# One change in six parts to an attention and mixer kernel: per-pair mixer, FFN halves queued apart, program order for two batches, mask by matmul, loads by need

## The chip, the core and the metric

The kernel runs on one core of a Trainium2 chip. The metric is the device time of one execution in microseconds (us). Every timed run carries a state, fast or slow (slow: over 1.5% above the fastest of its kernel), and only fast runs are compared. "Before" and "after" are the kernels without and with the change; e1 to e18 are experiments.

## The reference, cut to what matters

Eight batches, eight heads, 576 positions, head size 64. Attention with a causal mask and a bias from a running sum comes first. Its output is laid out as `x` (576 x 512 for each batch). A low-rank mixer along the sequence and a two-layer FFN follow.

```python
scores = q @ k.T * scale + min(bias, 0)        # causal: -1e9 above the diagonal
attn   = softmax(scores)
x      = (attn @ v).transpose(0, 2, 1, 3).reshape(B, S, H * D)
u      = x + ((x.T @ U) @ V).T                  # U: 576 x 32, V: 32 x 576
out    = u + relu(u @ w_ch1) @ w_ch2            # 512 -> 2048 -> 512
```

## The kernel before

Work is cut into 32 head pairs, four to a batch, and nine FFN blocks of 512 tokens. For each pair `scores(n)` makes the exponentials and `values(n)` the attended values in `x_sb`. Once per batch `seqmix(b)` turns `x_sb` into `u`, held transposed as `uT`. `chanmix(g)` is one FFN block: a wide half (`relu(u @ w_ch1)`) and a narrow half. The FFN is the filler. It waits in a queue, and one of its steps is put after each step of attention, so that TensorE (PE) has something to do while the others work on the softmax.

Queries and keys of pairs 4 and up come in groups of two pairs. A group is loaded by GpSimd's queue into `qk_sd`, then `place(g)` turns it: four stream transposes on VectorE (DVE) into `turned`, then eight copies by DMA into a slot. This is called "the turn". Group g serves pairs 2g and 2g+1.

```python
def place(g):                                   # "the turn" of group g
    slot = slots[g % NSLOT]
    nc.sync.dma_start(out=slot[D:KA, ...], in_=rows_hbm[...])
    src = qk_t.pop(g)
    turned = work.tile([128, 2, 2, S], BF16, tag="turned", name="turned")
    for e in range(2):
        for c in range(2):
            nc.vector.transpose(turned[:, e, c]..., src[:, c]...)          # L172, 4 in all
        for a in range(4):
            nc.sync.dma_start(out=slot[ds(32 * e, 32), a, 0 : 2 * S], ...)  # L177, 8 in all

def seqmix(b):                                  # once per batch
    x_sb = x_of.pop(b)
    up = pwork()
    for t in range(5):
        nc.tensor.matmul(up, lhsT=U_sb[:, t, :], rhs=x_sb[:, t, :], ...)   # L266, 512 columns
    ux = work.tile([128, DM], BF16, tag="ux", name="ux")
    nc.vector.tensor_copy(ux, up)
    yield
    for dt in range(4):
        ...                                     # x_sb transposed + V.T @ ux, then copied to uT
        yield
    ...

    # the end of the program: the opening is in program order, the rest is not
    with tc.manual_schedule():
        ...                                     # loads, set-up, batch 0, spin matmuls (48)
        warmly(seqmix(0))
    place(2)
    fill.append(chanmix(0))
    fill_with(8)
    for n in range(PB, NP + 1):                 # PB = 4 pairs in a batch, NP = 32
        b, hp = divmod(n, PB)
        if hp == 0 and b + 1 < B:
            load_qk(b + 1)
            load_v(b + 1)
        if hp % 2 == 0 and n + 2 < NP:
            place(n // 2 + 1)                   # two pairs ahead
        if n < NP:
            run(scores(n))                      # one filler step after each step
        if n > PB:
            run(values(n - 1))
            if hp == 0:
                run(seqmix(b - 1))
                fill.append(chanmix(b - 1))
    ...
```

Inside `tc.manual_schedule()` every engine gets its instructions in the order of the program. Outside, a scheduler chooses the order on each engine when the kernel is built. "Program order" means the former, "the scheduler" the latter. The spin matmuls are useless ones that keep PE busy in the opening.

The softmax here doesn't subtract the row's maximum and nothing guards it: scores larger than these inputs give would overflow.

Of the kernel before, what the change touches and what calls it, by code (L numbers as in the profile page):

```python
# [20 lines left out]
def kernel(  # L21
# [52 lines left out]
    identity = consts.tile([128, 128], BF16)  # L74
    PW = 1664
# [26 lines left out]
    def load_qk(b):  # L102
        for g in range(2 * b, 2 * b + 2):
            qk_t[g] = loads.tile([128, 2, ST * D], BF16, tag="qk_sd", name="qk_sd", bufs=3)
            for c, src in enumerate((q, k)):
                for a in range(4):
                    nc.gpsimd.dma_start(  # L107
                        out=qk_t[g][ds(32 * a, 32), c, :].rearrange("p (n f) -> p n f", n=6),
                        in_=src[b, 4 * (g % 2) + a].rearrange("(n p t) d -> p n (t d)", p=32, t=3),
                    )  # L110
# [71 lines left out]
    def scores(n):  # L182
        pT = pTs[n % 2]
        tail = pscore()
        for hh in range(2):
            qT = head_of(n, hh)[0:KA, 0:S]
            kT = head_of(n, hh)[0:KA, S:]

            def mm(dst, j, lo, hi):
                nc.tensor.matmul(  # L190
                    dst,
                    lhsT=kT[:, ds(j * 128, 128)],
                    rhs=qT[:, lo:hi],
                    start=True,
                    stop=True,
                )

            diag = pscore()
            for j in range(4):
                mm(diag[:, ds(j * 128, 128)], j, j * 128, j * 128 + 128)  # L200
            nc.scalar.activation(pT[:, hh, 0:512], diag, EXP, scale=scale)  # L201
            nc.vector.tensor_tensor(  # L202
                pT[:, hh, 0:512], pT[:, hh, 0:512], keep.rearrange("p a b -> p (a b)"), op=ALU.min
            )
            mm(tail[:, ds(hh * 64, 64)], 4, 512, S)
            yield
            far = pscore()
            mm(far[:, 0:448], 0, 128, S)
            mm(far[:, 448:512], 3, 512, S)
            nc.scalar.activation(pT[:, hh, 512:1024], far, EXP, scale=scale)  # L210
            mid = pscore()
            mm(mid[:, 0:320], 1, 256, S)
            mm(mid[:, 320:512], 2, 384, S)
            nc.scalar.activation(pT[:, hh, 1024:1536], mid, EXP, scale=scale)  # L214
            if hh == 1:
                nc.scalar.activation(
                    pT[:, :, 1536:1600],
                    tail[:, 0:128].rearrange("p (a b) -> p a b", a=2),
                    EXP,
                    scale=scale,  # L220
                )
                nc.vector.tensor_tensor(  # L222
                    pT[:, :, 1536:1600], pT[:, :, 1536:1600], keep[:, 0:2, 0:64], op=ALU.min
                )
            yield
# [36 lines left out]
    def seqmix(b):  # L262
        x_sb = x_of.pop(b)
        up = pwork()
        for t in range(5):
            nc.tensor.matmul(  # L266
                up,
                lhsT=U_sb[:, t, :],
                rhs=x_sb[:, t, :],
                start=(t == 0),  # L270
                stop=(t == 4),
            )
        ux = work.tile([128, DM], BF16, tag="ux", name="ux")
        nc.vector.tensor_copy(ux, up)
        yield
        for dt in range(4):
            ut = pwork()
            for t in range(4):
                nc.tensor.matmul(  # L279
                    ut[:, ds(t * 128, 128)],  # L280
                    lhsT=x_sb[:, t, ds(dt * 128, 128)],
                    rhs=identity,
                    start=(t == 0),
                    stop=False,
                    skip_group_check=True,
                )
            nc.tensor.matmul(  # L287
                ut,
                lhsT=ux[:, ds(dt * 128, 128)],
                rhs=V_sb[:, 0:512],  # L290
                start=False,
                stop=True,
                skip_group_check=True,
            )
            nc.vector.tensor_copy(uT[:, dt, ds(b * S, 512)], ut)  # L295
            yield
        ut = pwork()
        for dt in range(4):
            nc.tensor.matmul(
                ut[:, ds(dt * 64, 64)],  # L300
                lhsT=x_sb[:, 4, ds(dt * 128, 128)],
                rhs=identity[:, :64],
                start=True,
# [3 lines left out]
            nc.tensor.matmul(  # L307
                ut[:, ds(dt * 64, 64)],
                lhsT=ux[:, ds(dt * 128, 128)],
                rhs=V_sb[:, 512:S],  # L310
                start=False,
                stop=True,
                skip_group_check=True,
            )
        nc.vector.tensor_copy(
            uT[:, :, ds(b * S + 512, 64)], ut[:, 0:256].rearrange("p (a b) -> p a b", a=4)
        )
        yield

# [3 lines left out]
    def chanmix(g):  # L323
        hT = work.tile([128, NF, 512], BF16, tag="hT", name="hT")
        for nf in range(NF):
# [10 lines left out]
            yield  # L336
        for i in range(4):
# [36 lines left out]
    def run(gen):  # L374
        for _ in gen:
            step_fill()
# [8 lines left out]


    copy_a, copy_v = nc.scalar.copy, nc.vector.tensor_copy
    with tc.manual_schedule():
# [4 lines left out]
        load_first(4, 4)  # L393
        nc.gpsimd.memset(keep, 3.0e38)
# [9 lines left out]
        ones(warm)  # L404
        ones(rows[:, 0:3, 0, :])
        ones(rows[:, 3, 1, :])
        for slot in slots:
            nc.vector.memset(slot[:KA, :, 2 * S :], 0.0)
        idle = pwork()

        def spin(n):
            for _ in range(n):
                nc.tensor.matmul(idle, lhsT=warm[:, 0:128], rhs=warm, start=True, stop=True)  # L413

        spin(10)
        chain = first_transposes(0, (copy_a, copy_a))
        nc.vector.tensor_scalar(s_sb, s_sb, 0.0, 1.0 / scale, op0=ALU.max, op1=ALU.mult)
        nc.vector.tensor_tensor_scan(cum, s_sb, s_sb, 0.0, op0=ALU.add, op1=ALU.max)
        next(chain)
        spin(2)  # L420
        nc.scalar.mul(rows[:, 3, 0, :], cum, -1.0)
        drain(chain)
        spin(2)
        rest = s_sb
        nc.vector.tensor_copy(rows[:, 0, 1, :], cum)
        nc.vector.tensor_sub(rest, cum, rows[:, 0, 1, :])
        nc.vector.tensor_copy(rows[:, 1, 1, :], rest)
        nc.vector.tensor_sub(rows[:, 2, 1, :], rest, rows[:, 1, 1, :])
        for h in range(H):
            nc.sync.dma_start(  # L430
                out=slots[h // 4][D:KA, h % 4, 0 : 2 * S],
                in_=rows[h : h + 1].rearrange("n r c s -> n r (c s)"),
            )
        nc.sync.dma_start(
            out=rows_hbm[:, ds(2 * PB, BH - 2 * PB)].rearrange("r n c s -> n r c s"),
            in_=rows[2 * PB :],
        )
        for i, vt in enumerate(v_slots):
            nc.vector.memset(vt[:, :, :, D : D + 1], 1.0)
            nc.vector.memset(vt[64:, 4, :, :], 0.0)  # L440
            if i == 0:
                drain(first_transposes(1, (copy_a, copy_v)))
                spin(8)
        nc.vector.memset(U_sb, 0.0)
        nc.vector.memset(V_sb, 0.0)
        for pT in pTs:
            nc.vector.memset(pT[:, :, 1600:], 1.0)
        load_v(0)
        nc.gpsimd.dma_start(
            out=U_sb[:, :4, :R], in_=moe_U[:512].rearrange("(kt kp) r -> kp kt r", kp=128)  # L450
        )
        nc.gpsimd.dma_start(out=U_sb[:64, 4, :R], in_=moe_U[512:576])
        nc.gpsimd.dma_start(out=V_sb[:R], in_=moe_V)
        load_w1(0)
        load_w1(1)
        load_qk(1)
        load_w1(2)
        load_w1(3)
        load_v(1)
        for i in range(4):  # L460
            load_w2(i)
# [4 lines left out]

        drain(scores(0))
        warmly(first_transposes(2, (copy_v, copy_v)))
        drain(scores(1))
        warmly(first_transposes(3, (copy_v, copy_v)))  # L470
        warmly(values(0))
        warmly(scores(2))
        warmly(values(1))
        warmly(scores(3))
        warmly(values(2))
        warmly(values(3))
        warmly(seqmix(0))
    place(2)
    fill.append(chanmix(0))
    fill_with(8)  # L480
    for n in range(PB, NP + 1):
        b, hp = divmod(n, PB)
        if hp == 0 and b + 1 < B:
            load_qk(b + 1)
            load_v(b + 1)
        if hp % 2 == 0 and n + 2 < NP:
            place(n // 2 + 1)
        if n < NP:
            run(scores(n))
        if n > PB:  # L490
            run(values(n - 1))
            if hp == 0:
                run(seqmix(b - 1))
                fill.append(chanmix(b - 1))
    fill.append(chanmix(NG - 1))
    while fill:
        step_fill()
# [30 lines left out]
```

## Time and profile before

| | before |
|---|---|
| time, median of the first 3 runs | 410.95 us (409.07 to 414.25) |
| span of the profiled run | 409.0 us |
| PE busy, weight loads busy | 94%, 52% |
| spin matmuls | 48, 20.6 us busy |

The page cuts the span into 40 slices of about 10 us. Each digit is a busy share in tenths; PEclk is the clock that PE was granted, in tenths of full speed.

```profile
PE   7885999976998999999999999999999999999996
...
DVE  6759514778677455654675733442444331002011
...
PEclk9886899995999999999999999999999999999999
DMA  8999999999997967292147311220011002001002
```

PE is full from the eleventh slice on. Whatever can be won lies in the first 100 us. The busy table by stretch says it in numbers. Its columns are the stretch, its length, then busy us of PE, weight loads, DVE, ACT and POOL with instruction counts, the granted clock, the DMA engines' share and GB/s.

```profile
0.00:46.00 46.00, 35.65 (x328) 20.78 (x329) 33.94 (x71) 19.62 (x36) 30.00 (x49) 0.81 1.19 147
46.00:60.00 14.00, 14.00 (x90) 7.19 (x89) 3.37 (x8) 10.55 (x21) 4.54 (x8) 1.00 1.78 185
60.00:80.00 20.00, 18.96 (x176) 10.99 (x175) 13.35 (x25) 11.41 (x24) 13.53 (x22) 1.00 1.59 153
80.00:102.00 22.00, 15.28 (x158) 9.80 (x156) 15.84 (x31) 6.30 (x15) 17.19 (x29) 0.77 1.62 213
102.00:405.00 303.00, 300.14 (x2464) 165.12 (x2461) 128.87 (x263) 144.80 (x283) 45.39 (x71) 1.00 0.41 68
```

From 102 us on PE idles 303.00 - 300.14 = 2.9 us. From 80 to 102 us it idles 6.7 us and is granted 0.77 of its clock. PE's timeline (start, duration, engine, line, what it does, number of instructions, and in brackets the idle time before it with what ended it) shows the FFN's start, pair 4's scores, and the longest wait:

```profile
46.49 7.07 PE L328 MATMUL pwork<-uT,w_sb 128*128 128x512 bf16 x32
53.39 0.42 PE L190 MATMUL pscore<-slot 68*128 68x128 bf16 x5
...
95.80 2.29 PE L266 MATMUL pwork<-x_sb,U_sb 128*128 128x512 bf16 x5 [4.40 <-DVE x_sb L253]
```

DVE's timeline shows where the turns (L172) stand. Groups 2 and 3 are both turned by 48 us, interleaved with batch 0's last work. The later ones wait, for a load at 66.52 and at 84.16 for the slot copies of an earlier turn:

```profile
30.97 2.10 DVE L172 STREAM_TRANSPOSE turned<-qk_sd 128x576 bf16<-128x576 bf16 x2 [3.49 <-DMA qk_sd<-in_q_dram]
...
47.18 1.12 DVE L172 STREAM_TRANSPOSE turned<-qk_sd 128x576 bf16<-128x576 bf16 x1
...
66.52 2.10 DVE L172 STREAM_TRANSPOSE turned<-qk_sd 128x576 bf16<-128x576 bf16 x2 [6.17 <-DMA qk_sd<-in_q_dram]
...
84.16 2.11 DVE L172 STREAM_TRANSPOSE turned<-qk_sd 128x576 bf16<-128x576 bf16 x2 [4.37 <-DMA slot<-turned]
```

### The profile page before, as it was taken

The numbers are of one execution on the slowest core, as the hardware profiler recorded it, in microseconds if no ns is written. First come the engines' busy times: TensorE is split into PE (matmuls) and PEld (weight loads), VectorE is DVE, ScalarE is ACT, GpSimd is POOL, SyncE is SP. The second block draws the span as 40 slices with busy tenths as digits, with TensorE's granted clock in tenths as the row PEclk, the third lists the DMA queues.
The fourth block names the chain that finished last, engine by engine and source line by source line (L and its number), as shares of the span: only waits on it lengthen the run. The fifth ranks groups of instructions, "written<-read, shape, count | busy, mean of one in ns | idle before, by whom it ended". The sixth has DMA issues, their size and how long they took to land.

```text
span 409.0 us, 8107 instructions
## 1 busy us (share of the span) xinstructions
PE 384.1 (94%) x3208; PEld 213.9 (52%) x3208; DVE 196.1 (48%) x396; ACT 192.7 (47%) x376; POOL 110.6 (27%) x177
## 2 busy tenths in 40 slices
PE   7885999976998999999999999999999999999996
PEld 3553455543555555555555555565555554444442
DVE  6759514778677455654675733442444331002011
ACT  5751296350773187327742684358336630630710
POOL 7739326688872714260030000000000000000000
PEclk9886899995999999999999999999999999999999
DMA  8999999999997967292147311220011002001002
GB/s 116 152 147 137 170 220 146 168 227 194 168 147 111 158 112 106 64 167 75 42 55 99 99 35 30 69 69 2 2 51 53 2 0 79 26 27 58 20 27 77
DMA packets 78572, 37.91 MB, mean 93 GB/s; under 512 B 64518, under 2 KB 69798, under 8 KB 78534
## 3 DMA queue, kind: packets, MB, share of 16 engines
q0 software_dynamic: 67312, 18.44, 50.1%
q1 hardware_dynamic: 11222, 18.96, 15.8%
q8 instruction: 25, 0.41, 0.4%
q14 instruction: 13, 0.11, 0.1%
HBM read 37.51 MB, written 9.95 MB: 116 GB/s over the span
## 4 chain that ended last, share of the span: by engine, by line
PE 70%; DVE 13%; DMA 10%; issue 3%; POOL 2%; ACT 2%; DVEq 0%; ACTq 0%; SPq 0%; POOLq 0%
PE pwork L328 26%; PE pwork L341 24%; DVE turned L172 8%; PE pscore L190 7%; PE pwork L243 4%; DMA qk_sd<-in_q_dram 3%; PE pwork L266 3%; DMA v_slot<-in_v_dram 2%; PE pwork L287 2%; DMA U_sb<-in_moe_U_dram 2%; PE pwork L279 2%; DVE x_sb L253 2%; DMA slot<-turned 2%; PE pwork L352 2%; POOL qk_sd L107 1%
## 5 line engine op out<-in xcount | busy, mean ns | idle before, releaser
L341 PE MATMUL pwork<-w_sb,hT 128*128 128x512 bf16 x576 | 142.0, 379 | 0.4 <-DVE o_sb L361 0.4
L328 PE MATMUL pwork<-uT,w_sb 128*128 128x512 bf16 x576 | 141.5, 379 | 0.3 <-DVE x_sb L253 0.3
L335 ACT ACTIVATE hT<-pwork 128x512 bf16<-128x512 f32 x144 | 88.9, 618 | 83.4 <-PE pwork L328 82.5
L201 ACT ACTIVATE pT<-pscore 128x512 bf16<-128x512 f32 x64 | 39.0, 609 | 89.0 <-PE pscore L190 89.0
L341 PEld LDWEIGHTS <-hT 128*128 128x128 bf16 x576 | 52.2, 98 | 48.3 <-issue 0.5
L328 PEld LDWEIGHTS <-w_sb 128*128 128x128 bf16 x576 | 51.2, 98 | 46.5 <-DVE x_sb L253 0.8
L190 PE MATMUL pscore<-slot 68*128 68x128 bf16 (+4 forms) x576 | 66.8, 242 | 1.2 <-ACT pT L201 0.6
L172 DVE STREAM_TRANSPOSE turned<-qk_sd 128x576 bf16<-128x576 bf16 x56 | 59.8, 1120 | 15.3 <-DMA qk_sd<-in_q_dram 10.2
L361 DVE COPY o_sb<-pwork 128x512 f32<-128x512 f32 x36 | 24.7, 687 | 79.2 <-PE pwork L352 79.2
L190 PEld LDWEIGHTS <-slot 68*128 68x128 bf16 x576 | 43.7, 98 | 32.6 <-issue 3.2
L202 DVE TENSOR_TENSOR pT<-pT,keep 128x512 bf16<-128x512 bf16 x64 | 26.6, 418 | 58.2 <-ACT pT L201 58.2
L243 PEld LDWEIGHTS <-pT 128*128 128x128 bf16 x960 | 38.7, 100 | 22.0 <-issue 4.6
L243 PE MATMUL pwork<-v_slot,pT 128*128 128x65 bf16 x960 | 41.5, 197 | 7.8 <-DVE pT L222 2.9
L210 ACT ACTIVATE pT<-pscore 128x512 bf16<-128x512 f32 x64 | 39.5, 617 | 11.3 <-PE pscore L190 11.3
L214 ACT ACTIVATE pT<-pscore 128x512 bf16<-128x512 f32 x64 | 39.9, 623 | 9.5 <-PE pscore L190 9.5
L107 POOL DMA_DIRECT2D qk_sd<-in_q_dram x56 | 31.8, 587 | 30.4 <-DVE rec L252 11.2
L107 POOL DMA_DIRECT2D qk_sd<-in_k_dram x56 | 31.7, 575 | 26.4 <-DMA w_sb<-in_moe_w_ch_dram 12.3
L115 POOL DMA_DIRECT2D v_slot<-in_v_dram x32 | 28.2, 901 | 38.7 <-PE pwork L243 37.1
L253 DVE TENSOR_TENSOR x_sb<-pwork,rec 128x320 bf16<-128x320 f32 x64 | 31.2, 488 | 2.1
L295 DVE CAST uT<-pwork 128x512 bf16<-128x512 f32 x32 | 21.5, 685 | 12.2 <-PE pwork L287 12.2
L252 DVE RECIPROCAL rec<-pwork 128x5 f32<-128x5 f32 x64 | 11.6, 181 | 24.9 <-PE pwork L243 24.8
L413 PE MATMUL pwork<-warm 128*128 128x512 bf16 x48 | 20.6, 504 | 1.3 <-DVE warm L91 1.3
(53 smaller groups left out, 173.2 us busy)
## 6 DMA issues: line engine op xcount, KB each, us to landing
out_dram<-o_sb SPq DMA_DIRECT2D x36, 256.0 KB
slot<-turned SPq DMA_DIRECT2D x112, 72.0 KB
v_slot<-in_v_dram POOLq DMA_DIRECT2D x32, 128.0 KB, 5.3
w_sb<-in_moe_w_ch_dram POOLq DMA_DIRECT2D x8, 512.0 KB, 13.5
qk_sd<-in_q_dram POOLq DMA_DIRECT2D x56, 72.0 KB, 4.7
qk_sd<-in_k_dram POOLq DMA_DIRECT2D x56, 72.0 KB, 4.3
v_slot<-in_v_dram POOLq DMA_DIRECT2D x8, 64.0 KB, 6.0
rows_hbm<-hT SPq DMA_DIRECT2D x1, 504.0 KB
```

The source lines that it names most:

```text
L107: nc.gpsimd.dma_start(out=qk_t[g][ds(32 * a, 32), c, :].rearrange("p (n f) -> p n f", n=6), in_=src[b, 4 * (g % 2) + a].rearrange("(n p t) ...
L115: nc.gpsimd.dma_start(out=vt[:, t, :, 0:D], in_=v[b, :, ds(t * 128, 128), :].rearrange("h p d -> p h d"),)
L172: nc.vector.transpose(turned[:, e, c].rearrange("p (n m t) -> p n t m", n=6, t=3), src[:, c].rearrange("p (n t e d) -> p e n t d", n=6, t= ...
L190: nc.tensor.matmul(dst, lhsT=kT[:, ds(j * 128, 128)], rhs=qT[:, lo:hi], start=True, stop=True,)
L201: nc.scalar.activation(pT[:, hh, 0:512], diag, EXP, scale=scale)
L210: nc.scalar.activation(pT[:, hh, 512:1024], far, EXP, scale=scale)
L214: nc.scalar.activation(pT[:, hh, 1024:1536], mid, EXP, scale=scale)
L243: nc.tensor.matmul(po[:, i, :], lhsT=pT[:, hh, ds(spot(j, i), 128)], rhs=vt[:, j, h, :], start=(j == 0), stop=(j == i), skip_group_check=True,
L253: nc.vector.tensor_tensor(x_sb[:, :, ds(h * D, D)], po[:, :, 0:D], rec.to_broadcast([128, 5, D]), op=ALU.mult,)
L328: nc.tensor.matmul(f1, lhsT=w1_sb[nf // 4][:, kt, ds(nf % 4 * 128, 128)], rhs=uT[:, kt, ds(g * 512, 512)], start=(kt == 0), stop=(kt == 3),)
L335: nc.scalar.activation(hT[:, nf, :], f1, RELU)
L341: nc.tensor.matmul(f2, lhsT=hT[:, nf, ds(i * 128, 128)], rhs=w2_sb[nf // 4][:, nf % 4, :], start=(nf == 0), stop=False, skip_group_check=True,
```

## The change

The intent is to start the FFN earlier and then never to let PE stand. (1) The mixer runs per pair (`mix`), so less hangs on a batch's last pair. (2) The FFN's halves are queued apart (`widen`, `narrow`), so a wide half needs no `w_ch2`. (3) Batches 0 and 1 are in program order. (4) Batch 0's causal mask is added to the scores by a matmul instead of being cut by DVE. (5) Loads are ordered by need, and a group is loaded on its own. (6) Spins fall from 48 to 16, and batch 1 takes filler at 0.4 steps for each step of its own. The core of the diff, with cuts:

```diff
-    def seqmix(b):
+    def mix(n, copy=None):
+        b, hp = divmod(n, PB)
+        x_sb, cols = x_of[b], ts(hp, 128)
         up = pwork()
         for t in range(5):
-            nc.tensor.matmul(up, lhsT=U_sb[:, t, :], rhs=x_sb[:, t, :], ...)
-        ux = work.tile([128, DM], BF16, tag="ux", name="ux")
-        nc.vector.tensor_copy(ux, up)
+            nc.tensor.matmul(up[:, 0:128], lhsT=U_sb[:, t, :], rhs=x_sb[:, t, cols], ...)
+        ux = work.tile([128, 128], BF16, tag="ux", name="ux")
+        nc.vector.tensor_copy(ux, up[:, 0:128])
...  # four transposes of x_sb, one of 64 columns, yield, two matmuls on ux, two copies to uT
-    def chanmix(g):
+    def widen(g):
...
+    def narrow(g):
...  # scores(): for n < PB a matmul `hide` adds -1e30 above the diagonal; `cut` (DVE) otherwise
+    def attend(n, rate):
+        b, hp = divmod(n, PB)
+        if n < NP:
+            run(scores(n), rate)
+        if n > PB:
+            run(values(n - 1), rate)
+            run(mix(n - 1), rate)
+            if hp == 0:
+                fill.append(widen(b - 1))
...
+    def second():                               # batch 1
+        fill.append(widen(0))
+        place(2)
+        fill_with(6)
+        load_qk(4)
+        load_v(2)
+        for i in range(3):
+            load_w2(i)
+        load_qk(5)
+        load_w2(3)
+        attend(4, 0.4)
+        place(3)
+        attend(5, 0.4)
+        attend(6, 0.4)
+        place(4)
+        attend(7, 0.4)
+        fill_with(16)
...
+    with tc.manual_schedule():
+        opening()                               # batch 0
+        second()
+    rest()
```

## The prediction

> **What bounds the kernel now.** The page gives PE 94% busy. The busy table by stretch shows where the rest is: from 102 us on PE idles only about 3 us, before that it idles or burns warm-up matmuls. The timeline gives the pitch of useful work: 0.86 us for four 128x512 FFN matmuls, 0.25 + 0.44 us for a head's scores, 0.46 us for its values, 3.1 us for a batch's mixer. Summed, useful PE work is about 357 us (estimate from these). Of it about 56 us is done by 102 us, so about 46 us of the 409 is lost there: the first FFN matmul starts at 46.5 us, and PE stands again at 85 to 96 us (the waits show the mixer's first matmul waiting 8.3 us for x_sb, 4.4 us once). The causes are on DVE and DMA: DVE's in-order stream has q/k stream transposes (1.12 us each) ahead of batch 0's x_sb writes, and stands for their loads (6.4 and 6.2 us idle at 48 to 67 us, the second ended by a q load). Software DMA runs at 100 to 190 GB/s until 100 us; a V batch lands in about 6 us, a 512 KB weight piece in 2.6, a q/k group in 3.2 (spacing of landings).
>
> **What the change does.** Useful matmul columns stay the same; the mask adds 8 matmuls of 512 and 4 of 128 columns (about 2 us) in the opening and takes about 1.06 us of DVE per pair of batch 0 away. Spin matmuls fall from 48 to 16. In program order batch 0 finishes without q/k transposes in front. My chain: scores at about 11 us (12.9 before), exps 3.2 us per pair, FFN from about 38 to 42 us (46.5 before). One new wait: DVE's set-up of the second V tile comes after its load, about 36 us. Batch 1 then runs against DVE (about 31 us with four groups' transposes) and ACT (about 22 us).
>
> The limit after that is loads. The sixth q/k group stands behind the third V batch and three w2 pieces; it landed at 72.6 us before, I estimate 73 to 79 us now. Pair 10's scores follow at 80 to 88 us; PE is dense from there. By then it has done about 44 us of useful work, leaving 313, plus 6 us of small waits and the last store: 399 to 407 us, or about 394 if the loads run faster. From then on the per-pair mixer waits for x_sb four times as often as before (2.5 us in total after 102 us before); I allow 1 to 4 us. The tail is unchanged: PE-bound, same work.
>
> **Prediction: 399 us, 390 to 409 in 8 of 10. Faster by over 2%: 0.62; within 2%: 0.35; slower: 0.03.**
>
> **What would show it.** First FFN matmul at 38 to 42 us; DVE transposes after batch 0's last x_sb; PE dense from 75 to 88 us, its last long wait ended by DVE transposes or a q/k load; spins about 7 us instead of 20; PE busy time lower, idle before 100 us smaller but not gone. [...]
>
> **What would make it wrong.** Loads slower than I reckon [...], so pair 10 comes after 90 us: no gain. More x_sb waits in steady state. [...] On the other side, if DMA was not the limit, dense from 70 us: about 390 us.

The forecast's sum: 80 to 88 us until pair 10's scores, 313 us of work left and 6 us of waits and the last store come to 399 to 407 us. Two readings in it differ from before's trace: only the 6.17 us idle of DVE was ended by a load, the 6.41 us one by ACT's `pT`; and the software DMA queue moved 89 to 151 GB/s in each 10 us up to 100 us, all queues together 114 to 244.

## The result, and the profile after

| | before | after |
|---|---|---|
| time, median of 4 runs | 410.4 us (409.07 to 414.25) | 425.87 us (425.61 to 426.89) |
| span of the profiled run | 409.0 us | 423.9 us |
| PE busy, weight loads busy | 384.1 us (94%), 52% | 386.5 us (91%), 52% |
| mean granted clock | 0.966 | 0.954 |

The ratio is 1.037 (95% interval 1.029 to 1.044): the change costs 15 us. Every ratio in this document is the mean time of one kernel's fast runs over the mean of the other's in the same rounds, so it is not quite the ratio of the medians quoted.

```profile
PE   6794786769999999999999999999999999999996
...
DVE  7565443779667685655747443344434101001011
...
PEclk9579868988999999999999999999999999999999
DMA  7999999899993996892291221001000201102001
```

Most of the first ten slices are emptier than before, the rest is as full. By stretch:

```profile
0.00:44.00 44.00, 30.53 (x329) 20.80 (x333) 28.29 (x62) 16.95 (x33) 30.88 (x52) 0.80 1.36 129
44.00:60.00 16.00, 12.41 (x53) 5.95 (x54) 4.48 (x8) 8.32 (x17) 11.01 (x17) 0.71 2.14 178
60.00:80.00 20.00, 14.36 (x146) 8.82 (x147) 10.14 (x24) 9.66 (x21) 8.10 (x14) 0.90 1.30 187
80.00:100.00 20.00, 14.24 (x146) 9.13 (x146) 17.46 (x35) 10.84 (x24) 11.50 (x18) 0.87 1.45 136
100.00:420.00 320.00, 314.96 (x2585) 175.75 (x2631) 137.17 (x308) 146.10 (x282) 49.91 (x79) 1.00 0.44 71
```

From 44 to 100 us PE idles 3.6 + 5.6 + 5.8 us (length minus busy), and the granted clock is 0.71, 0.90 and 0.87 where it was 1.00 from 46 to 80 us (before's 80 to 102 us had 0.77). After 100 us it idles 5.0 us in 320, a part of which may be missing matmul records. So the loss lies before 100 us. PE's timeline names the waits:

```profile
42.73 0.45 PE L286 MATMUL pwork<-x_sb,U_sb 128*128 128x128 bf16 x5 [3.77 <-DVE x_sb L271]
...
44.07 6.72 PE L339 MATMUL pwork<-uT,w_sb 128*128 128x512 bf16 x24
54.02 2.26 PE L205 MATMUL pscore<-slot 68*128 68x128 bf16 x14 [3.23 <-DMA slot<-turned]
...
70.46 1.28 PE L205 MATMUL pscore<-slot 68*128 68x128 bf16 x9 [3.16 <-DMA slot<-turned]
...
87.83 0.72 PE L286 MATMUL pwork<-x_sb,U_sb 128*128 128x128 bf16 x5 [4.33 <-DVE x_sb L271]
...
100.71 1.23 PE L205 MATMUL pscore<-slot 68*128 68x128 bf16 x9
```

The FFN starts 2.4 us earlier than before (44.07 against 46.49), not the 4.5 to 8.5 us predicted. Its 24 matmuls take 6.72 us at a mean granted clock of 0.79 (0.52 from 44 to 47 us, then 1.00), where 24 at before's pitch take 23 x 0.216 + 0.38 = 5.35 us (from before's 32, at a clock of 1.00: 7.07 less the last one's 0.38, over 31). Then PE waits 3.2 us for pair 4's turn, 3.2 us for pair 6's, and 4.3 us for `x_sb`. DVE, and the queue (SPq) that issues the slot copies, show why:

```profile
40.80 0.49 DVE L528 MEMSET v_slot<- 64x520 bf16 x1 [0.17 <-DVE v_slot L527]
...
42.18 0.49 DVE L271 TENSOR_TENSOR x_sb<-pwork,rec 128x320 bf16<-128x320 f32 x1
...
43.43 4.00 DVE L172 STREAM_TRANSPOSE turned<-qk_sd 128x576 bf16<-128x576 bf16 x4
...
59.98 4.03 DVE L172 STREAM_TRANSPOSE turned<-qk_sd 128x576 bf16<-128x576 bf16 x4
...
80.19 4.04 DVE L172 STREAM_TRANSPOSE turned<-qk_sd 128x576 bf16<-128x576 bf16 x4
...
84.95 1.09 DVE L172 STREAM_TRANSPOSE turned<-qk_sd 128x576 bf16<-128x576 bf16 x1
```

```profile
45.54 5.03 SPq L177 DMA_DIRECT2D slot<-turned  x8
...
62.13 4.96 SPq L177 DMA_DIRECT2D slot<-turned  x8
```

The four transposes for pair 4 begin at 43.43, right behind batch 0's last `x_sb` (before: at 30.97), though their data had landed at 28.6 us. With the eight copies the turn takes 54.02 - 43.43 = 10.6 us until pair 4's scores. The next turn starts only at 59.98, behind pair 4's mask cuts; its scores come at 70.46. By the landing records of the trace (as all landings here) its data had been there since 42.5 us. The group for pair 8 landed at 54.4 us and was turned from 80.19 on, the one for pair 10 at 76.3 us and was turned from 84.95 on. The data was there; the turn was not. Pair 10's scores, at 100.71, show no wait of their own: the last copy of their turn was issued by 92.5 us, and they stand in PE's order behind pairs 8 and 9 (from 91.19 on), whose delay they inherit.

A count of useful work shows when the loss happens. Each weight load of the scores, values and FFN that has begun by time t counts with the pitch of its matmul at a granted clock of 1.00 (0.216 us in the FFN, 0.69/9 in the scores, 0.031 in the values). Weight loads are used because matmul records can be missing; the page after has 548 + 552 = 1100 of the FFN's 1152 matmuls, and all its weight loads.

| useful us begun by | 60 us | 100 us | 120 us | 300 us |
|---|---|---|---|---|
| before | 23.0 | 48.8 | 67.4 | 224.6 |
| after | 17.7 | 36.4 | 52.8 | 209.3 |
| e1 | 18.7 | 47.0 | 60.1 | 217.4 |
| e9 | 18.2 | 47.3 | 64.5 | 224.5 |
| e11 | 24.7 | 56.2 | 75.9 | 235.8 |
| e15 | 22.5 | 51.0 | 68.2 | 222.2 |

After is 14.6 us behind before at 120 us and 15.3 us behind at 300 us. The whole loss is there by 120 us.

The granted clock differs by stretch. In after it is 0.50 from 10 to 21 us, where PE is busy 8.2 of 11 us and waits 2.5 us for DMA, and 0.71 in the stretch with the first wait for a turn. From 100 us on, where PE is busy 315 of 324 us, it is 1.00. But from 30 to 44 us, where PE is busy only 7.9 of 14 us, it is 0.98. What lowers it was not tested.

### The profile page after: what moved, and what is told of

Same layout as the page of the kernel before. It is cut to its first block, busy times and chain, and to the rows that moved or that the text cites. A ratio compares the mean times of both kernels' runs of the same rounds, so it can differ in the third digit from the quotient of the medians.

```text
span 423.9 us, 8293 instructions
## 1 busy us (share of the span) xinstructions
PE 386.5 (91%) x3252; PEld 220.4 (52%) x3308; DVE 198.2 (47%) x433; ACT 191.9 (45%) x375; POOL 111.4 (26%) x179
## 3 DMA queue, kind: packets, MB, share of 16 engines
q1 hardware_dynamic: 11222, 18.96, 15.3%
## 4 chain that ended last, share of the span: by engine, by line
PE 65%; DMA 19%; POOL 6%; DVE 4%; issue 3%; SPq 1%; DVEq 0%; POOLq 0%
PE pwork L355 26%; PE pwork L339 23%; DMA w_sb<-in_moe_w_ch_dram 6%; PE pscore L205 6%; DMA v_slot<-in_v_dram 5%; PE pwork L261 4%; DMA qk_sd<-in_k_dram 4%; DMA qk_sd<-in_q_dram 3%; DVE turned L172 3%; POOL qk_sd L107 3%; PE pwork L286 2%; PE pwork L366 2%; POOL v_slot L115 2%; PE pwork L315 1%; DMA slot<-turned 1%
## 5 line engine op out<-in xcount | busy, mean ns | idle before, releaser
L339 PE MATMUL pwork<-uT,w_sb 128*128 128x512 bf16 x548 | 143.8, 390 | 1.8 <-issue 0.4
L355 PE MATMUL pwork<-w_sb,hT 128*128 128x512 bf16 x552 | 138.1, 379 | 1.2
L346 ACT ACTIVATE hT<-pwork 128x512 bf16<-128x512 f32 x144 | 87.7, 610 | 112.3 <-PE pwork L339 112.2
L205 PE MATMUL pscore<-slot 68*128 68x128 bf16 (+4 forms) x576 | 71.8, 254 | 10.9 <-DMA slot<-turned 6.4
L339 PEld LDWEIGHTS <-w_sb 128*128 128x128 bf16 x576 | 52.5, 100 | 52.4 <-issue 7.7
L219 ACT ACTIVATE pT<-pscore 128x512 bf16<-128x512 f32 x64 | 38.8, 606 | 76.1 <-PE pscore L205 62.4
L198 DVE TENSOR_TENSOR pT<-pT,keep 128x512 bf16<-128x512 bf16 (+1 forms) x84 | 27.4, 350 | 48.7 <-ACT pT L219 44.4
L227 ACT ACTIVATE pT<-pscore 128x512 bf16<-128x512 f32 x64 | 39.0, 610 | 12.0 <-PE pscore L205 11.9
L261 PEld LDWEIGHTS <-pT 128*128 128x128 bf16 x960 | 37.4, 99 | 11.6 <-issue 0.2
L261 PE MATMUL pwork<-v_slot,pT 128*128 128x65 bf16 x960 | 40.0, 195 | 0.0
L231 ACT ACTIVATE pT<-pscore 128x512 bf16<-128x512 f32 x64 | 39.4, 616 | 0.0
L286 PE MATMUL pwork<-x_sb,U_sb 128*128 128x128 bf16 x160 | 14.6, 223 | 13.4 <-DVE x_sb L271 13.3
```

The costliest lines, as they stand in the source:

```text
L205: nc.tensor.matmul(dst, lhsT=kT[:, ds(j * 128, 128)], rhs=qT[:, lo:hi], start=start, stop=stop, skip_group_check=not stop,)
L219: nc.scalar.activation(pT[:, hh, 0:512], diag, EXP, scale=scale)
L227: nc.scalar.activation(pT[:, hh, 512:1024], far, EXP, scale=scale)
L231: nc.scalar.activation(pT[:, hh, 1024:1536], mid, EXP, scale=scale)
L261: nc.tensor.matmul(po[:, i, :], lhsT=pT[:, hh, ds(spot(j, i), 128)], rhs=vt[:, j, h, :], start=(j == 0), stop=(j == i), skip_group_check=True,
L339: nc.tensor.matmul(f1, lhsT=w1_sb[nf // 4][:, kt, ds(nf % 4 * 128, 128)], rhs=uT[:, kt, ds(g * 512, 512)], start=(kt == 0), stop=(kt == 3),)
```

## The experiments

Eighteen kernels, each with the reference's outputs. The kernel before was timed in every group of runs; its median lay between 409.9 and 411.2 us, so medians of different groups are compared too. T1: batch 1's program order puts each turn on the path ("Theory A" in the expectations). T2: the per-pair mixer costs time of its own. The rivals: the loads are late ("Theory B", the prediction's own story), or batch 1 has too little filler ("Theory E"). T2 came up only with e6, from which I expected little.

### e1: the turns ahead, nothing else

```diff
@@ after, second() @@
         place(2)
+        place(3)
         fill_with(6)
...
         attend(4, 0.4)
-        place(3)
+        place(4)
         attend(5, 0.4)
         attend(6, 0.4)
-        place(4)
         attend(7, 0.4)
```

> The changed kernel with its second and third q/k turns of batch 1 and 2 (place(3), place(4)) moved up: place(3) straight after place(2), place(4) straight after pair 4. Theory A (program order puts the transposes and the slot writes, about 10 us from first transpose to landing, on the critical path of batch 1 although their loads landed at 42.5 and 54.4 us): pair 6's scores start at about 66 us, not 70.5; pair 8's at 82 to 86, not 91.2; PE dense 6 to 10 us earlier; 416 to 420 us instead of 425.9. Theory B (loads set the pace, as the prediction had it): pair 8 stays at about 90 us and the time within 2 us of 425.9.

Measured: 416.74 us, ratio to before 1.016 (1.012 to 1.020). Two moved lines give back 9.1 of the 15 us. Pair 6's scores start at 65.56 instead of 70.46 and wait for no turn. T1 is shown. What remains are waits for `x_sb`, 7.2 us in six waits from 44 to 120 us. Pair 6's scores and the longest of these waits in PE's timeline, then DVE's:

```profile
65.56 0.85 PE L205 MATMUL pscore<-slot 68*128 68x128 bf16 x9
...
106.39 0.71 PE L286 MATMUL pwork<-x_sb,U_sb 128*128 128x128 bf16 x5 [3.10 <-DVE x_sb L271]
```

```profile
103.30 1.14 DVE L172 STREAM_TRANSPOSE turned<-qk_sd 128x576 bf16<-128x576 bf16 x1 [2.57 <-DMA qk_sd<-in_q_dram]
104.30 0.46 DVE L271 TENSOR_TENSOR x_sb<-pwork,rec 128x320 bf16<-128x320 f32 x1
```

At 106.39 the mixer's first matmul has waited 3.10 us for `x_sb`. DVE writes `x_sb` only at 104.30, though the reciprocal that it uses was done at 100.74: a transpose stands in front, and that one waits 2.57 us for a load.

### e2: batch 1 given to the scheduler

```diff
@@ after @@
     with tc.manual_schedule():
         opening()
-        second()
+    second()
     rest()
```

> The changed kernel with only the opening (batch 0) in program order; batch 1 given to the scheduler as in the kernel before. Theory A: transposes move up in DVE's order, the waits of PE scores for the slot writes (3.2 us twice) go, 412 to 420 us. Theory B: 423 to 427 us. If it is as slow as the changed kernel, the program order of batch 1 is not the cause.

Measured: 420.12 us, ratio 1.023 (1.019 to 1.027). The time is 5.8 us less than after's and in the range that T1 gave, but the reason given for it did not come true: PE's waits for turns did not go. They are 7.0 us in three waits (longest 4.5), against 6.4 in two in after, and the FFN starts only at 57.37 us, behind pair 4's scores. So e2 shows that this order was costly, but not that the turns were the cost; that rests on e1.

### e3: the sixth group's load first

```diff
@@ after, second() @@
         load_qk(4)
+        load_qk(5)
         load_v(2)
-        for i in range(3):
+        for i in range(4):
             load_w2(i)
-        load_qk(5)
-        load_w2(3)
```

> The changed kernel with the sixth q/k group loaded before the third V batch and all of w2. Theory B: pair 10's scores come 6 to 12 us earlier, 416 to 421 us. Theory A: the group lands at about 58 instead of 76 us and nobody uses it sooner; 424 to 428 us.

Measured: 427.09 us, ratio 1.040 (1.037 to 1.043), where after's is 1.037. Pair 10's group landed at 57.7 us instead of 76.3, and that wins nothing. The load story is rejected: with the turns where after has them, loads are not the limit. Whether they become it once the turns are early was not run.

### e4: more filler in batch 1

```diff
@@ after, second() and rest() @@
-        load_v(2)
-        for i in range(3):
+        for i in range(4):
             load_w2(i)
+        load_v(2)
         load_qk(5)
-        load_w2(3)
-        attend(4, 0.4)                  # likewise 5, 6, 7
+        fill.append(narrow(0))
+        attend(4, 1.0)
...
-            if n == 2 * PB:
-                fill.append(narrow(0))
```

> The changed kernel with w2 loaded right after the fifth q/k group and the narrowing half of FFN group 0 (64 matmuls of 512 columns and 16 of 128, about 14.7 us) queued as filler in batch 1, one step a yield instead of 0.4. Theory E (the waits of batch 1 stay, but PE had nothing to fill them with, since the w2 pieces were put off and the filler thinned): pair 8's scores come at 91 to 96 us with 14.7 us more work done, 412 to 419 us. If the filler only pushes the chain back, 423 us or more.

The 14.7 us are an estimate from before's pitches: 64 matmuls of 0.216 us and four groups of four that take 0.23 us each (85.14 to 85.37).

Measured: 426.07 us median, but two of four runs (427.05, 427.14) were slow by the 1.5% rule (their clocks, 0.956 and 0.952, do not stand apart), and the fast ones are 420.3 and 425.1. The ratio of the fast runs is 1.029 (1.022 to 1.036). Two runs 4.8 us apart decide nothing: inconclusive.

### e5: e1 and e4 together

> The early turns of e1 and the filler of e4 together (w2 straight after the fifth q/k group, narrowing half of group 0 as filler at one step a yield). Theory A with E: with the turns out of the pairs' way the filler no longer pushes the chain back, so its 14.7 us of work falls into waits: 404 to 411 us. If the filler still pushes the chain back (DVE, ACT and loads are the limit), 414 to 418 us, no better than e1 alone (416.7).

The edit is e1's and e4's. Measured: 426.81 us, ratio 1.040 (1.034 to 1.047), 10 us worse than e1 and outside both expected ranges. Two things differ from e1, the filler and the place of the `w2` loads, now ahead of the third V batch. Pair 4's scores start at 58.1 us (e1: 52.92) before any added filler has run: PE waits 5.2 us for the turn's slot copies (e1: 1.49). From 60 to 80 us PE is full (19.68 of 20 us), yet the pairs come later and later, pair 10's scores at 115.8 (e1: 87.5). By the count of useful work e5 is level with e1 at 100 us (47.1 against 47.0) and 4.3 us behind at 120. So the added work filled the gaps, but the pairs came later, and nothing was won. Which of the two edits costs the 10 us was not separated.

### e6: the per-pair mixer alone, in the kernel before

```diff
@@ before @@
+    def mix(n, copy=None):              # as in after
...
-        warmly(seqmix(0))
+        for n in range(4):
+            warmly(mix(n))
...
             run(values(n - 1))
+            run(mix(n - 1))
             if hp == 0:
-                run(seqmix(b - 1))
                 fill.append(chanmix(b - 1))
```

> The kernel before with the mixer per head pair, nothing else. Work counted in the traces of before and after keeps a constant distance from 120 us on (14.6 us, then 15.4 and 15.3), so I expect the mixer to cost little: 409 to 413 us. If the mixer's four times as many waits for x_sb matter, 414 us or more; if it helps because the FFN's input is ready sooner, under 408.

Measured: 417.01 us, ratio 1.016 (1.008 to 1.023): 7 us for the mixer alone, where I had expected 409 to 413 us. That the mixer costs time (T2) is shown. DVE's timeline, then PE's, show the largest wait:

```profile
67.70 1.13 DVE L172 STREAM_TRANSPOSE turned<-qk_sd 128x576 bf16<-128x576 bf16 x1 [9.77 <-DMA slot<-rows_hbm]
68.69 0.19 DVE L222 TENSOR_TENSOR pT<-pT,keep 128x128 bf16<-128x128 bf16 x1
```

```profile
68.94 0.34 PE L243 MATMUL pwork<-v_slot,pT 128*128 128x65 bf16 x3 [5.29 <-DVE pT L222]
```

PE waits 5.29 us for a mask cut of 0.19 us, which stands behind a transpose for which DVE had idled 9.77 us. From such lines I formed the theory that the per-pair mixer hurts only because it makes the scheduler place turns badly. e13 to e15 test that.

### e7 and e8: two parts alone, in the kernel before

e7 queues the FFN's halves apart. e8 puts batch 1 in program order, with the turns where before has them, two pairs ahead.

```diff
@@ e7, before @@
-    def chanmix(g):
+    def widen(g):                       # and narrow(g), as in after
...
-                fill.append(chanmix(b - 1))
+                fill.append(widen(b - 1))
+                if b == 2:
+                    fill.append(narrow(0))
+                fill.append(narrow(b - 1))
@@ e8, before: one(n) is the body of the loop @@
+    with tc.manual_schedule():
+        place(2)
+        fill.append(chanmix(0))
+        fill_with(8)
+        for n in range(PB, 2 * PB):
+            one(n)
+    for n in range(2 * PB, NP + 1):
+        one(n)
```

> The kernel before with the FFN halves queued apart, nothing else: the narrowing half of group 0 waits until pair 8. Theory E (PE loses the 14.7 us of filler it had at 63 to 85 us): PE idles there, and 416 to 425 us. If instead the chain of loads, turns and exps then runs sooner by as much as PE is freed, 408 to 413 us.

> The kernel before with batch 1 in program order too, its turns called ahead of the scores as its loop has them (place(3) before pair 4, place(4) before pair 6), nothing else. Theory A as I now hold it (it is the place of the turns in that order, not program order as such): 407 to 413 us. If program order as such costs, 416 us or more.

Measured: e7 410.7 us, ratio 1.002 (0.995 to 1.008); e8 409.34 us, ratio 0.999 (0.992 to 1.006). Both do nothing. e8 sharpens T1: program order in batch 1 costs nothing when the turns stand ahead. The fault is the place of the turns.

### e9 and e10: the batch mixer back

e10 is after with `mix(n - 1)` in `attend` replaced by before's `seqmix(b - 1)` once per batch, from batch 1 on. Batch 0 keeps the per-pair mixer. e9 is e1 with the same edit.

```diff
@@ after, attend() @@
             run(values(n - 1), rate)
-            run(mix(n - 1), rate)
             if hp == 0:
+                run(seqmix(b - 1), rate)
                 fill.append(widen(b - 1))
```

> e1 (turns moved up) with the mixer once per batch from batch 1 on, as in the kernel before. My theory now is two causes that add: T1, the turns sit behind the pairs in batch 1's program order (about 9 us, e1), and T2, the per-pair mixer makes PE wait at every pair for x_sb, which DVE's in-order stream holds behind q/k transposes (about 7 us, e6). Both undone: 408 to 412 us, level with the kernel before. If T2 is not it, 415 to 418, as e1.

> The changed kernel with only the mixer back to once per batch from batch 1 on, turns left late. T2 alone undone: 417 to 421 us. If the two causes do not add (the late turns already hold everything), 424 to 427.

Measured: e10 422.03 us, ratio 1.025 (1.021 to 1.030), 3.8 us less than after. e9 410.39 us, ratio 0.997 (0.994 to 1.001), 6.4 us less than e1. With both causes undone the kernel is level with before. So T1 and T2 account for the whole loss against before: 9.1 and 3.8 us when undone alone, 15.5 us together. They do not simply add.

### e11: the kernel before, all in program order

```diff
@@ before: one(n) is the body of the loop @@
+    with tc.manual_schedule():
+        place(2)
+        fill.append(chanmix(0))
+        fill_with(8)
+        for n in range(PB, NP + 1):
+            one(n)
+        fill.append(chanmix(NG - 1))
+        while fill:
+            step_fill()
```

> The kernel before, all batches in program order, turns two pairs ahead as its loop has them, so that the scheduler can put no transpose ahead of work whose load has landed. If scheduler-placed transposes that wait for loads hold DVE (4.4 us of idle before one at 84 us, PE idle at 85 to 97 us): 402 to 408 us. If loads and DVE's work are the limit there, 408 to 413. If program order costs overlap later, over 414.

Measured: 399.09 us (396.45 to 400.26), ratio 0.970 (0.964 to 0.975), faster than both kernels. The table of DVE's waits between 60 and 110 us (what waited, for what: total us, times, longest), for before and then for e11:

```profile
DVE turned L172 <- DMA qk_sd<-in_q_dram: 6.7, 2, 6.2
DVE turned L172 <- DMA slot<-turned: 4.4, 1, 4.4
```

```profile
DVE turned L172 <- DMA qk_sd<-in_q_dram: 1.2, 1, 1.2
...
DVE turned L172 <- DMA qk_sd<-in_k_dram: 0.4, 1, 0.4
```

In the kernel before DVE stands 11.1 us in front of transposes whose data or buffer is not ready; in e11 it is 1.6 us. The turn had a good place in the source, two pairs ahead, and the scheduler had moved it forward: the transposes for pairs 10 and 12 begin at 72.3 and 84.2 us in before and at 79.8 and 99.3 in e11. So after turned too late, and before too early, in front of work that was ready (in before the exponentials that begin at 61.56 were done at 62.34 and their mask cut ran at 68.48, behind the transposes that had waited 6.17 us). That the turns alone make e11's gain was not isolated, since e11 fixes every order. The work table says that 8.5 of e11's 11 us are won by 120 us.

### e12: the per-pair mixer one pair later

```diff
@@ e1, attend() and rest() @@
-            run(mix(n - 1), rate)
-            if hp == 0:
-                fill.append(widen(b - 1))
+            if n - 2 >= PB:
+                run(mix(n - 2), rate)
+            if n == NP:
+                run(mix(n - 1), rate)
...
-            if hp == 0:
+            if hp == 1 or n == NP:
+                fill.append(widen(b - 1))
                 fill.append(narrow(b - 1))
```

> e1 with the per-pair mixer run one pair later, so that a pair's scores and fillers lie between x_sb and the mixer that reads it (widen follows one pair later too). T2: PE's waits for x_sb fall from 11.8 us to under 5, 408 to 413 us. If the mixer's cost is its own work and not the wait, 415 to 418.

Measured: 413.78 us, ratio 1.006 (1.003 to 1.010), 3.0 us less than e1. Slack on `x_sb` gives back about half of what e9 gives. From 44 to 120 us no wait for `x_sb` is left (7.2 us in e1), but PE now waits for DVE's copy `ux` instead: 6.6 us in four waits (0.5 in e1). The longest in PE's timeline:

```profile
80.47 0.21 PE L306 MATMUL pwork<-identity,x_sb 128*128 128x64 bf16 x1 [3.39 <-DVE ux L295]
```

The same wait, L288 there, is what e15 shows below.

### e13, e14 and e15: is it the scheduler?

Each puts the whole program in order: e13 is e1, e14 is e9, e15 is e11 with the per-pair mixer. In e13 and e14 the edit is one line; e15 adds e6's edit to e11.

```diff
@@ e13 and e14 @@
         second()
-    rest()
+        rest()
```

> e1 with batches 2 to 7 in program order too, so everything is; the mixer stays per pair. If T2 (the per-pair mixer's cost) comes only through transposes that the scheduler puts ahead of x_sb before their loads have landed, as the 3.1 us wait at 103 us of e1 shows, program order takes it away: 398 to 406 us. If the mixer's waits are there in any order, 409 to 416.

> e9 (turns early, mixer per batch) with batches 2 to 7 in program order. With the opening of the change and e11's order: 396 to 402 us. Against e13 it gives what the per-pair mixer costs in program order: if T2 comes only through the scheduler's order, the two lie within 3 us; if it is the mixer's own, e13 is 5 us or more slower.

> e11 (the kernel before, all in program order, 399.1 us) with the mixer per pair. T2 only through the scheduler's order: 397 to 402 us. Mixer's own cost: 404 to 408, the 7 us of e6 again.

Measured: e13 425.92 us (1.036, 1.031 to 1.042); e14 408.46 us (0.995, 0.990 to 1.000); e15 416.16 us (1.014, 1.009 to 1.020). With no scheduler at all the per-pair mixer costs 17.5 us (e13 against e14) and 17.1 us (e15 against e11). My theory that it hurts only through the scheduler falls: without the scheduler it hurts more, and all three times lie outside what I had expected. PE's timeline in e15, at a place where nothing else is short, then DVE's:

```profile
162.11 1.03 PE L378 MATMUL pwork<-uT,w_sb 128*128 128x512 bf16 x4
163.09 0.45 PE L268 MATMUL pwork<-x_sb,U_sb 128*128 128x128 bf16 x5
163.38 0.39 PE L280 MATMUL pwork<-identity,x_sb 128*128 128x128 bf16 x4
163.93 0.19 PE L288 MATMUL pwork<-identity,x_sb 128*128 128x64 bf16 x1 [0.16 <-DVE ux L277]
163.95 1.02 PE L391 MATMUL pwork<-w_sb,hT 128*128 128x512 bf16 x4
```

```profile
163.58 0.29 DVE L277 CAST ux<-pwork 128x128 bf16<-128x128 f32 x1 [0.55 <-PE pwork L268]
```

Ends of matmuls are modelled, so starts are read here. Four FFN matmuls at 162.11 fill 0.86 us, to 162.97; the mixer's first matmul starts at 163.09, 0.12 us later, behind `x_sb`. Four transposes by matmul start at 163.38 and fill about 0.22 us (an estimate: they have as many columns as one FFN matmul of 0.216 us; after four like ones at 168.60 in the same trace the next instruction starts 0.23 us later); the next instruction starts at 163.93, about 0.33 us later, behind DVE's copy `ux` (0.29 us). That instruction does not use `ux`. It puts the last 64 columns of `x_sb` into other columns of the PSUM tile `up`, which the copy is reading. In the source no filler step stands between the matmuls on `U_sb` and this one, so nothing fills the gap. The trace shows the wait and that the copy ended it; that the shared tile is the reason is my reading and was not shown, for no run here gave the 64 columns a tile of their own. PE's table of waits for e15 from 120 to 380 us counts it 22 times; in the same stretch of e11 the table is empty:

```profile
PE pwork L288 <- DVE ux L277: 4.1, 22, 0.5
```

The table counts only what lies beyond the modelled ends. Read from the starts of matmuls, as above, the gap before the 64 columns adds up to 7.8 us over the 22 mixers between 120 and 380 us, and the gap before the mixer's first matmul to 2.8: 10.6 us, about 0.5 us for each. In e11 the gap before the mixers' first matmuls is 0.5 us in all in that stretch. The work table gives the rest its place: e15 is already 7.7 us behind e11 at 120 us (13.6 at 300).

### e16 and e17: the mask by matmul

e16 is before with batch 0's mask by matmul, as the change has it; e17 is e11 with the same edit, a candidate for the best version.

```diff
@@ before, scores() @@
+            if on_pe:                   # n < PB
+                hide(diag, 4)
             nc.scalar.activation(pT[:, hh, 0:512], diag, EXP, scale=scale)
-            nc.vector.tensor_tensor(pT[:, hh, 0:512], pT[:, hh, 0:512], keep..., op=ALU.min)
+            if not on_pe:
+                cut(pT[:, hh, 0:512], keep.rearrange("p a b -> p (a b)"))
```

> The kernel before with only batch 0's mask added by a matmul. It puts about 2 us on PE and takes 4.2 us from DVE in the opening, where DVE's transposes and x_sb writes follow each other: 406 to 411 us. Over 412 would make it a third cause of the loss.

> e11 (the kernel before, all in program order, 399.1 us) with batch 0's mask added by a matmul: the one part of the change that e16 showed harmless, where the opening's DVE stream is now the limit. 397 to 400 us if it is as neutral as in e16; under 396 if the opening is bound by DVE's masks.

Measured: e16 409.62 us, ratio 0.997 (0.993 to 1.002); e17 398.37 us (396.70 to 398.52), ratio 0.968 (0.963 to 0.973). Alone the mask is neutral. e17 is the fastest kernel run, though its lead over e11 is within the spread of both; that DVE is the limit of e11's opening, as the expectation says, was not shown.

### e18: e14 with more filler

The edit is e4's, in e14.

> e14 (opening of the change, turns early, mixer per batch, all in program order, 408.5 us) with w2 loaded straight after the fifth q/k group and the narrowing half of group 0 as filler in batch 1 at one step a yield. e14 is 9 us slower than e11 and by its trace 5.8 us behind at 60 us and 10.6 at 80 us. If the 5 us from 60 to 80 us are the missing filler: 402 to 405 us. If the chain of batch 1 sets the pace anyway (as e4, e5 and e7 say): 407 to 411 us.

Measured: 405.48 us median of four runs, one of them slow (410.39); the fast ones are 404.23, 404.36 and 406.6; ratio of the fast runs 0.986 (0.980 to 0.991). With the turns ahead and the batch mixer, filler (with the earlier `w2` loads) helps by 3 to 4 us, where it harmed in e5. e14 is 9 us behind e11, and this gives back a third or more.

## Why the prediction was wrong, point by point

The prediction was 399 us, with 3% for slower; the kernel took 425.87. Its reading of the kernel before held: the loss lies before 102 us, and DVE's stream (11.1 us of idle in front of transposes from 60 to 110 us) and the place of the turns in it are behind it. What failed is the cost of what the change put in its place.

1. **"The limit after that is loads." "Pair 10's scores follow at 80 to 88 us; PE is dense from there."** This is the step that failed. The load was sized rightly: 73 to 79 us predicted, 76.3 measured. But pair 10's scores came at 100.71. Between a group's landing and its scores stand the turn and its place in DVE's order, and the prediction had no term for either. A turn takes 10.6 us (43.43 to 54.02). In program order the turns for pairs 4, 6 and 8 started behind work that was not needed first (43.43, 59.98, 80.19), and the scores of these pairs came at 54.02, 70.46 and 91.19, so pair 10's came late in their wake. e1 puts the missing term at 9.1 us; e3 shows that an earlier load wins nothing. "PE is dense from there" failed too, and e1 shows it apart from the date: there pair 10's scores start at 87.5 us, inside the predicted window, and the time is still 416.7. By a count of all useful matmuls at the same pitches (an estimate, mixers included), 45 us of 355 were done when pair 10's scores began, in after as in e1, which fits the predicted 44. The remaining 310 us of work then took 324 us in after and 328 in e1, where the prediction allowed 6 us on top, and 1 to 4 for `x_sb`. e9, which takes the per-pair mixer out of e1, wins 6.4 us of this (point 3).

2. **"In program order batch 0 finishes without q/k transposes in front."** This came true, and was counted as pure gain. The transposes had to be done all the same. Before, two turns were done by 48 us in the shade of batch 0; after, the first began at 43.43 and the FFN's 24 matmuls (44.07 to 50.79) could not cover it. I wrote "about 31 us with four groups' transposes" for DVE, which counts their durations and not what waits behind them.

3. **"From then on the per-pair mixer waits for x_sb four times as often ... I allow 1 to 4 us."** The kind was right, the size too small. The mixer costs 3.8 us in after (e10), 6.4 in e1 (e9), 7 in before (e6) and 17 in pure program order (e13, e15). I counted waits for `x_sb` only. The wait for DVE's copy `ux`, which I put down, untested, to the last 64 columns sharing a PSUM tile with what the copy reads, was not in my sum; in program order it is the larger gap, 0.33 us of about 0.5 for a pair (e15). After 100 us the waits for `x_sb` in after are 2.0 us, against 2.5 in before: the steady state is not where it shows there.

4. **The FFN's start at 38 to 42 us.** It came at 44.07. The last mixer matmul of batch 0 waited 3.77 us for `x_sb`, which stood behind the set-up of the V tiles; I had named that wait ("DVE's set-up of the second V tile comes after its load, about 36 us") but let it end too early. So the gain over before was 2.4 us, and the turn took it back at once.

5. **The other signs.** The spins took 7.1 us (right), transposes came after batch 0's last `x_sb` (right), and the last long wait, 4.33 us, was for `x_sb` behind transposes (right in kind, at 87.83). PE busy rose to 386.5 us instead of falling: 13.5 us of spins went, but by line the mask's matmuls add 5.1 us, the mixer's 64-column and first matmuls 9.3 and the scores 5.0. Idle before 100 us grew from about 18 us (to 102) to about 28.5. The first 24 FFN matmuls took 1.4 us more than at before's pitch (6.72 against 5.35).

What the experiments leave open: e14, which has after's opening with both faults removed and all in program order, is still 9 us behind e11. e18 gets 3 to 4 us of it back by filler and earlier `w2` loads. At 60 us e14's count of useful work is 18.9 us and e11's 24.7, and PE's granted clock from 40 to 60 us is 0.74 in e14 and 0.95 in e11. Whether the fewer spins, the later first turn or the opening's order is to blame was not separated: no run changed the spins alone. Also open is the per-pair mixer's cost: 10.6 of its 17 us in program order were placed, and whether a tile of its own for the 64 columns would save most of that was not tried.

The parts that do nothing by themselves: the halves queued apart (e7), program order in batch 1 with early turns (e8), the mask (e16). The new load order was not tested by itself; e3 moves one load within it. The version to keep is e17: before, all in program order, turns two pairs ahead, mask by matmul, 398.37 us.

## What to carry to other kernels

When a change fixes the order by hand, follow each chain from "data has landed" to "first matmul that reads it", and start its first link as soon as the data is there, ahead of work that is needed later: here two moved lines were worth 9 us, while an earlier load was worth nothing. Cutting a small chain of matmul, copy, matmul into four times as many pieces can add open waits even where the columns stay the same: here PE waited 22 times for the copy between 120 and 380 us in e15 and not once in e11. Look at which tiles the pieces share, though that this was the reason was not tested. And test the old kernel with the new order alone: that experiment, not the change, gave the 3%.
